# Two of the 32 exponentials in each attention block, computed on VectorE by a polynomial

## The chip, the cores and the metric

The kernel runs on one core of one Trainium2 chip. The metric is the device time of one execution in microseconds (us), the lower the better. Three runs of the kernel before took 1523.89, 1523.95 and 1524.58 us; the median is 1523.95 us. A separate execution was recorded by the hardware profiler; all instruction times below are from that one.

## The reference, cut to what matters

Two attention layers over 2048 tokens with 32 heads of 18 dimensions; their outputs are put side by side.

```python
# A: 32 query heads, one shared key head and one shared value head, no mask
q = (x @ wq) -> [32, 2048, 18];  k = x @ wk;  v = x @ wv            # k, v: [2048, 18]
p = softmax(q @ k.T * 18 ** -0.5);  a = (p @ v, heads joined) @ wo

# B: 32 full heads, four segments of 512 tokens, causal inside a segment
logits = qs @ ks.T * 18 ** -0.5 + mask;  p = softmax(logits)
o = g * (phi(qs) @ M) / (phi(qs) @ z) + (1 - g) * (p @ vs)           # M, z: from earlier segments
b = (o, heads joined) @ wo
out = concatenate([a, b], axis=-1)                                   # float32
```

The change concerns the exponential of A's softmax: 32 heads x 2048 queries x 2048 keys.

## The kernel before, in words

**Stages.** The first 330 us compute projections (queries, keys, values of A and B), bounds that are subtracted inside the exponentials, and B's memory; they write their results to DRAM. The rest, which the change is in, is the attention stage, then a short output stage.

**Blocks and pairs.** An A block is four heads (`hg`) of one chunk of 512 queries (`c`); there are 4 x 8 = 32 of them. Inside a block the loop runs over 16 tiles of 128 keys (`kt`) and, for each, over two *pairs* of heads (`pr`), so a block has 32 pairs. For one pair, `scores` (L715) issues two TensorE matmuls that run side by side on two halves of the rows (L726) and fill one PSUM tile `E` of 128 keys x 2 heads x 512 queries; then one ScalarE instruction (L727) takes the exponential of all 128 x 1024 values into an SBUF tile `P`. `products` (L747) multiplies `P` by the values: for one key tile and one half of the queries (`hf`) it issues four matmuls, one for each head, side by side in four column groups (L761). They add up in one PSUM tile `O`. The sums of the exponentials come out as an extra column of the values. A B block is the same with 3 key tiles, six pairs, narrower ones, and a GpSimd `affine_select` (L741) that cuts off the future.

**PSUM.** There are three `E` tiles (`psE`, L558), handed out in turn: pair i can be filled only when pair i-3 has been read. `O` and `F` have one tile each (`psO`, L559).

**Turns.** TensorE, ScalarE and VectorE execute in the order in which the program issues their work (L843); the order of DMAs on the SyncE queue (SP) and of GpSimd's work is left to the framework. The loop at L854 runs *turns*. A turn issues the scores (and exponentials) of three pairs, one step of the output projection (`run_fill(1)`: four matmuls, L648, into `F`), and the products that belong to the pairs of two turns before. An A block has ten turns of three pairs and one turn, the last, of two; a B block has two turns. There are 352 + 64 = 416 turns. After every fifth step of the projection VectorE copies `F` to SBUF (`osb`, L672), and TensorE needs that copy done before the next step. When a block's products are complete, VectorE copies `O` out (`oe`, L770), and TensorE needs that copy done before the next block's first products.

**Steps that follow a finished chunk.** When all heads of a chunk (A) or a segment (B) are through, `finish` (L801) puts a chain into the list `later`: read the sums back from DRAM (`sums`), take reciprocals on VectorE (`inverses`, L609), load the unnormalized heads and the broadcast reciprocals (`load_heads`, L615), multiply on VectorE (`weigh`, L628). When five such head groups are weighed, the chunk's output projection joins the list `fill`: 60 steps. `due` (L793) executes at most one entry of `later` in a turn. Eight projections are made; the steps that are left when the turns are over are executed after them (L876), and the last chunk's (L889, L895) after that.

## Time and profile before

| | |
|---|---|
| three runs, us | 1523.89, 1523.95, 1524.58 |
| the profiled execution, us | 1525.33 |
| its span on the core, us | 1523.6 |
| TensorE (PE) matmul busy | 1474.2 us, 97% of the span |
| ScalarE (ACT) busy | 1234.7 us, 81% |
| VectorE (DVE) busy | 316.6 us, 21% |
| GpSimd (POOL) busy | 119.3 us, 8% |
| granted TensorE clock | 0.992 over the whole span, 1.00 from 345 to 1480 us |
| window 400 to 1400 us: ACT busy | 98% (980.5 of 1000 us) |
| window 400 to 1400 us: DVE busy | 11% (114.0 of 1000 us) |

How to read it: a row of the group view names the line, the engine, the operation, the tiles written and read, and how often it ran; then the busy time of the group in us (overlaps counted once), the mean duration of one in ns, and the idle time of the engine ahead of the group with what ended it. ScalarE's instructions overlap a little, so their mean duration is longer than their spacing. "PEld" is the load of a matmul's weights, the first thing that a matmul does, so a wait of TensorE shows there. A float32 matmul stands as two instructions in the trace; the score matmuls as one. TensorE's busy share counts overlapped matmuls from start to modelled end and is no measure of its spare time. The timeline view gives start, duration, engine, line and, in brackets, the idle time before a row.

### The profile page before, as it was taken

The page shows a single profiled execution, that of the slowest core. Times are in us where ns is not written, and L with a number is a line of the kernel's source. Part 1 is how long each engine was busy: PE and PEld are TensorE (multiplying, and loading weights), DVE is VectorE, ACT ScalarE, POOL GpSimd, SP SyncE. Part 2 cuts the span into 40 slices and gives each one's busy share as a digit, 9 for nine tenths or more (in the row PEclk, how much of TensorE's full clock was granted, in tenths as well). Part 3 has the DMA queues.
Part 4 walks back from the last instruction along what each step waited for, and adds up shares of the span by engine and source line. Part 5 has one row for each costly group of instructions (what it writes and reads, how often), then busy time and mean ns, then how long its engine had stood idle before and what let it go on. Part 6 is the DMA issues. An engine that isn't in the chain of part 4 may idle for free.

```text
span 1523.6 us, 40356 instructions
## 1 busy us (share of the span) xinstructions
PE 1474.2 (97%) x17540; PEld 840.1 (55%) x17540; DVE 316.6 (21%) x607; ACT 1234.7 (81%) x1456; POOL 119.3 (8%) x221
## 2 busy tenths in 40 slices
PE   8989999999999999999999999999999999999998
PEld 5668878754444555545555454555554444444454
DVE  6564673530011001211000001112012100100011
ACT  3333334259999999999999999999999999999950
POOL 0030000002121111001001010111100000000000
PEclk9989999999999999999999999999999999999999
DMA  6775643456464243432332213342322111010011
GB/s 196 232 234 175 188 153 128 139 169 185 128 187 134 59 135 108 152 101 71 95 101 69 89 51 103 105 144 73 102 90 77 53 41 47 27 52 16 32 64 60
DMA packets 87983, 166.29 MB, mean 109 GB/s; under 512 B 12480, under 2 KB 21242, under 8 KB 87626
## 3 DMA queue, kind: packets, MB, share of 16 engines
q1 hardware_dynamic: 81510, 157.82, 33.4%
q10 hardware_dynamic: 6291, 5.85, 1.2%
q8 instruction: 138, 2.26, 0.6%
q14 instruction: 44, 0.35, 0.1%
HBM read 96.15 MB, written 67.49 MB: 107 GB/s over the span
## 4 chain that ended last, share of the span: by engine, by line
PE 64%; ACT 7%; DMA 3%; issue 3%; SPq 1%; DVE 0%; ACTq 0%; DVEq 0%
PE O L761 28%; PE E L726 21%; PE F L648 12%; ACT P L727 5%; PE E L734 3%; ACT P L737 2%; DMA stB<-qB 1%; PE E L648 1%; DMA woA<-a_wo 1%; DMA stB<-shB 0%; SPq L577 0%; DMA stA<-qA 0%; DVE osb L672 0%; DMA oB<-oe 0%; DMA stB<-ones_d 0%
## 5 line engine op out<-in xcount | busy, mean ns | idle before, releaser
L727 ACT ACTIVATE P<-E 128x1024 f32<-128x1024 f32 x1024 | 958.7, 1040 | 16.5 <-PE E L726 4.7
L761 PE MATMUL O<-P,VA 128*32 128x256 f32 x8192 | 509.3, 380 | 0.1
L726 PE MATMUL E<-stA,kstA 56*128 56x512 f32 x1920 | 367.7, 457 | 9.9 <-ACT P L727 7.4
L761 PEld LDWEIGHTS O<-P,VA 128*32 128x32 f32 x8192 | 261.4, 110 | 148.0 <-issue 10.1
L726 PEld LDWEIGHTS E<-stA,kstA 56*128 56x128 f32 x1920 | 154.4, 184 | 244.5 <-ACT P L727 239.1
L737 ACT ACTIVATE P<-E 128x768 f32<-128x768 f32 (+1 forms) x192 | 155.2, 898 | 8.4 <-PE E L734 7.2
L672 DVE COPY osb<-F 128x192 f32<-128x192 f32 x84 | 30.0, 358 | 594.9 <-PE F L648 594.9
L741 POOL TENSOR_SCALAR_AFFINE_SELECT P<-P 128x256 f32<-128x256 f32 (+1 forms) x192 | 94.6, 493 | 666.6 <-ACT P L737 663.4
L770 DVE COPY oe<-O 128x512 f32<-128x512 f32 x64 | 44.3, 692 | 405.5 <-PE O L761 348.8
L648 PE MATMUL F<-woB,o 126*32 126x192 f32 (+1 forms) x1920 | 127.0, 338 | 0.0
L648 PE MATMUL F<-woA,o 126*32 126x192 f32 (+2 forms) x1480 | 88.7, 337 | 6.1 <-DVE osb L672 6.1
L101 ACT CAST qp<-pj 126x512 fp32r<-126x512 f32 (+1 forms) x56 | 32.6, 584 | 64.7 <-DVE kmB L351 48.4
L761 PE MATMUL O<-P,vseg 128*32 128x256 f32 (+2 forms) x1536 | 81.5, 344 | 0.3 <-POOL P L741 0.2
L199 PE MATMUL pj<-xh,wBh 128*126 128x512 f32 x180 | 74.6, 419 | 3.4 <-DVE xh L171 3.4
L199 PE MATMUL pj<-xh,wBl 128*126 128x512 f32 x180 | 73.2, 406 | 0.0
L734 PE MATMUL E<-stB 56*128 56x256 f32 (+3 forms) x512 | 66.8, 354 | 5.6 <-ACT P L737 3.9
L648 PEld LDWEIGHTS F<-woB,o 126*32 126x32 f32 (+1 forms) x1920 | 38.5, 108 | 58.6 <-issue 53.8
L734 PEld LDWEIGHTS E<-stB 56*128 56x128 f32 x512 | 40.5, 184 | 40.7 <-ACT P L737 16.4
L761 PEld LDWEIGHTS O<-P,vseg 128*32 128x32 f32 x1536 | 48.2, 109 | 25.5 <-issue 2.7
L199 PE MATMUL pj<-xl,wBh 128*126 128x512 f32 x144 | 60.3, 419 | 0.0
L648 PEld LDWEIGHTS F<-woA,o 126*32 126x32 f32 (+1 forms) x1480 | 34.6, 108 | 43.6 <-issue 26.6
L102 DVE TENSOR_TENSOR qp<-pj,qp 126x512 fp32r<-126x512 f32 (+1 forms) x56 | 38.2, 686 | 55.7 <-ACT qp L101 55.5
(124 smaller groups left out, 998.7 us busy)
## 6 DMA issues: line engine op xcount, KB each, us to landing
stB<-kB SPq DMA_DIRECT2D x96, 144.0 KB
stB<-qB SPq DMA_DIRECT2D x32, 288.0 KB
stA<-qA SPq DMA_DIRECT2D x30, 288.0 KB
oA<-oe SPq DMA_DIRECT2D x32, 256.0 KB
oB<-oe SPq DMA_DIRECT2D x32, 256.0 KB
qA<-qp SPq DMA_DIRECT2D x16, 504.0 KB
kB<-qp SPq DMA_DIRECT2D x16, 504.0 KB
qB<-qp SPq DMA_DIRECT2D x16, 504.0 KB
```

Source lines behind the costliest of these rows:

```text
L101: nc.scalar.copy(qp[:R, 0, :n], src)
L102: nc.vector.tensor_tensor(qp[:R, 1, :n], src, qp[:R, 0, :n].bitcast(F32), op=ALU.subtract)
L199: nc.tensor.matmul(dst, w[:, c0 : c0 + M], x, start=i == 0, stop=i == len(ops) - 1)
L648: nc.tensor.matmul(dst[32 * j : 32 * j + 32], parts[ab, c][: RT[t], t, r0 : r0 + 32], wo[ab][: RT[t], t, c0 : c0 + n], start=start, stop=stop,
L672: nc.vector.tensor_copy(osb[:, cs], pf[:, :192])
L726: nc.tensor.matmul(e[:, j], kstA[rows, 128 * kt : 128 * kt + 128], st[rows, h, :], start=True, stop=True)
L727: nc.scalar.activation(p, e, AF.Exp, scale=SCALE)
L734: nc.tensor.matmul(e[:, j, c0 : c0 + 512 - 128 * k], st[rows, 4 + h, ks], st[rows, h, 128 * k :], start=True, stop=True)
L737: nc.scalar.activation(p[:, :, :n], e[:, :, :n], AF.Exp, scale=SCALE)
L741: nc.gpsimd.affine_select(diag, diag, pattern=[[0, 2], [0, m], [1, 128]], base=0, channel_multiplier=-1, compare_op=ALU.is_ge, fill=0.0)
L761: nc.tensor.matmul(o[32 * j : 32 * j + 32, q0 : q0 + n], v, ps_[j // 2][:, j % 2, p0 : p0 + n], start=kt == hf == 0, stop=kt == last and h ...
L770: nc.vector.tensor_copy(osb, o)
```

## The change

In each A block the pairs (key tile 1, pair 0) and (key tile 8, pair 1), numbers 2 and 17 of the block's 32 counted from 0, are taken from ScalarE. VectorE computes their exponential: one instruction reads `E`, scales by log2(e) and limits from below (this frees `E`), and eight more, on SBUF, round to an integer n, form the fraction, evaluate a polynomial of degree five, and multiply by 2^n, which is made from integer bits. The eight stand in a list `slow`, and the loop issues two in a turn, fewer when `due` executed something costly in that turn. The products of these pairs are put at positions 9 and 15 of the block's key order for that pair of heads (`LATE`); in pair 0 the products of key tiles 2 to 9 and in pair 1 those of key tiles 9 to 15 move one position ahead to fill the gap.

Beside this: the tiles of `load_heads` have three buffers instead of four and `vseg` one instead of two (its load is issued when the segment before has its last products); `due` executes up to two entries in a turn, one of them costly at most, and in turns of B too; heads are loaded one by one while fewer than three are held; the B blocks of segments 2 and 3 stand at other places among the A blocks (`after`).

```diff
@@ -42,6 +42,15 @@
 BKEYS = [[(0, 0)], [(1, 0)], [(2, 0), (3, 256)]]
 BHALF = [[(0, 0, 0, 256), (0, 256, 256, 256)], [(1, 0, 128, 192), (1, 192, 320, 192)], [(2, 0, 256, 256), (3, 256, 384, 128)]]
+
+
+LOG2 = SCALE * 1.4426950408889634
+ROUND = 1.5 * 2.0 ** 23
+POLY = [753.2113037109375, 522.0861206054688, 180.93731689453125, 41.808597564697266, 7.287727355957031]
+C5_BITS = 984482944.0
+
+BY_DVE = ((1, 0), (8, 1))
+LATE = (9, 15)
 QALL = [(slice(0, 36, 2), 0), (slice(1, 36, 2), 1), (slice(36, 54), 0)]
 CA = 618
@@ -614,9 +623,9 @@
     def load_heads(ab, c, t):
         o_d, r_d = (oA, rA) if ab == "A" else (oB, rB)
-        tiles = [pa.tile([128, C], F32, name=n, bufs=4) for n in ("oc", "rb")]
+        tiles = [pa.tile([128, C], F32, name=n, bufs=3) for n in ("oc", "rb")]
         if ab == "B" and c > 0:
-            tiles += [pa.tile([128, C], F32, name=n, bufs=4) for n in ("nb", "rb2")]
+            tiles += [pa.tile([128, C], F32, name=n, bufs=3) for n in ("nb", "rb2")]
         lo, n, R = H0[t], HT[t], RT[t]
         nc.sync.dma_start(tiles[0][:R], o_d[c][lo : lo + n, 1:VW, :])
         nc.sync.dma_start(tiles[1][:R], r_d[c][lo : lo + n, None, :].to_broadcast([n, DH, C]))
@@ -694,7 +703,7 @@
     blocksA = [("A", c, hg) for c in range(NCH) for hg in range(8)]
     blocksB = [[("B", s, 2 * h8), ("B", s, 2 * h8 + 1)] for s in range(NSEG) for h8 in range(4)]
-    after = [0, 0, 1, 1, 2, 3, 4, 5, 8, 10, 12, 14, 16, 17, 18, 19]
+    after = [0, 0, 1, 1, 2, 3, 4, 5, 8, 9, 10, 12, 16, 17, 18, 20]
     blocks = []
     for n, b in enumerate(blocksA):
         blocks.append(b)
@@ -707,10 +716,26 @@
     stacks, vseg, state = {}, {}, {}
     def load_vseg(s):
-        v = pa.tile([128, 4, H * VW + 13], F32, name="vseg", bufs=2)
+        v = pa.tile([128, 4, H * VW + 13], F32, name="vseg", bufs=1)
         nc.sync.dma_start(v[:, :, : H * VW], vB[s].rearrange("(i p) c -> p i c", p=128))
         nc.gpsimd.memset(v[:, :, H * VW :], 0.0)
         vseg[s] = v
+
+    slow = []
+
+    def exponentials(p, e):
+
+        n = pp.tile([128, 2, 512], F32, name="n", bufs=1)
+        q = pp.tile([128, 2, 512], F32, name="q", bufs=1)
+        v = nc.vector
+        v.tensor_scalar(p, e, LOG2, -116.0, op0=ALU.mult, op1=ALU.max)
+        slow.append((p, lambda: v.tensor_scalar(n, p, ROUND, ROUND, op0=ALU.add, op1=ALU.subtract)))
+        slow.append((p, lambda: v.tensor_tensor(p, p, n, op=ALU.subtract)))
+        slow.append((p, lambda: v.scalar_tensor_tensor(q, p, POLY[4], p, op0=ALU.add, op1=ALU.mult)))
+        for a in POLY[3:0:-1]:
+            slow.append((p, lambda a=a: v.scalar_tensor_tensor(q, q, a, p, op0=ALU.add, op1=ALU.mult)))
+        slow.append((p, lambda: v.tensor_scalar(n.bitcast(I32), n, 2.0 ** 23, C5_BITS, op0=ALU.mult, op1=ALU.add)))
+        slow.append((p, lambda: v.scalar_tensor_tensor(p, q, POLY[0], n, op0=ALU.add, op1=ALU.mult)))
     def scores(it, pr):
@@ -718,13 +743,17 @@
         st = stacks[ab, c, hg // 2]
         h = 2 * (hg % 2) + pr
         e = psE.tile([128, 2, 512], F32, name="E")
-        p = pp.tile([128, 2, 512], F32, name="P", bufs=PBUFS)
-        state.setdefault(it, []).append(p)
+        dve = ab == "A" and (kt, pr) in BY_DVE
+        p = pp.tile([128, 2, 512], F32, name="PD" if dve else "P", bufs=2 if dve else PBUFS)
+        state[it, pr] = p
         if ab == "A":
             for j, r0 in enumerate(HALF):
                 rows = slice(r0, r0 + KR)
                 nc.tensor.matmul(e[:, j], kstA[rows, 128 * kt : 128 * kt + 128], st[rows, h, :], start=True, stop=True)
-            nc.scalar.activation(p, e, AF.Exp, scale=SCALE)
+            if dve:
+                exponentials(p, e)
+            else:
+                nc.scalar.activation(p, e, AF.Exp, scale=SCALE)
             return
         n = 512 - 128 * kt if kt < 2 else 384
         for k, c0 in BKEYS[kt]:
@@ -744,16 +773,19 @@
     acc = {}
-    def products(it, hf):
-
-        ab, c, hg, kt = it
-        if kt == hf == 0:
+    def products(b, m, hf):
+
+
+        ab, c, hg = b
+        if m == hf == 0:
             acc[0] = psO.tile([128, C], F32, name="O")
         o = acc[0]
-        ps_ = state.pop(it) if hf else state[it]
-        last = NKT - 1 if ab == "A" else 2
-        k, p0, q0, n = (kt, 256 * hf, 256 * hf, 256) if ab == "A" else BHALF[kt][hf]
+        last = (NKT - 1 if ab == "A" else 2) == m
         for j in range(4):
+            kt = turn_of[j // 2][m] if ab == "A" else m
+            p = state[b + (kt,), j // 2]
+            assert all(x[0] is not p for x in slow)
+            k, p0, q0, n = (kt, 256 * hf, 256 * hf, 256) if ab == "A" else BHALF[kt][hf]
             if ab == "A":
                 v = VA[:, VW * kt : VW * kt + 32]
             else:
@@ -761,11 +793,11 @@
             nc.tensor.matmul(
                 o[32 * j : 32 * j + 32, q0 : q0 + n],
                 v,
-                ps_[j // 2][:, j % 2, p0 : p0 + n],
-                start=kt == hf == 0,
-                stop=kt == last and hf == 1,
+                p[:, j % 2, p0 : p0 + n],
+                start=m == hf == 0,
+                stop=last and hf == 1,
             )
-        if kt == last and hf:
+        if last and hf:
             osb = pa.tile([128, C], F32, name="oe", bufs=2)
             nc.vector.tensor_copy(osb, o)
             od = oA if ab == "A" else oB
@@ -773,6 +805,15 @@
             return hg
         return None
+
+    turn_of = []
+    for pr in range(2):
+        ks = [kt for kt in range(NKT) if (kt, pr) not in BY_DVE]
+        for (kt, p_), pos in zip(BY_DVE, LATE):
+            if p_ == pr:
+                ks.insert(pos, kt)
+        turn_of.append(ks)
+
     keys = {ab: list(dict.fromkeys((ab, c, hg // 2) for a_, c, hg in blocks if a_ == ab)) for ab in "AB"}
     def prefetch(ab, upto):
@@ -784,19 +825,22 @@
     prefetch("B", 1)
     load_vseg(0)
     FILL = 60
-    later, weighed, loaded = [], {}, [0]
-
-    def at(k, ready, step):
-        later.append((k, ready, step))
+    later, weighed, loaded, summing = [], {}, [0], set()
+
+    def at(k, cost, ready, step):
+        later.append((k, cost, ready, step))
         later.sort(key=lambda e: e[0])
-    def due(k, n=1):
-
+    def due(k, most=2):
+
+        cost = 0
         for e in [e for e in later if e[0] <= k]:
-            if n and e[1]():
+            if most and not (cost and e[1]) and e[2]():
                 later.remove(e)
-                e[2](k)
-                n -= 1
+                e[3](k)
+                cost += e[1]
+                most -= 1
+        return cost
     def finish(k, ab, c, hg):
@@ -805,22 +849,29 @@
         box = {}
         weighed.setdefault((ab, c), 0)
         last = (ab, c) == blocks[-1][:2]
-        d1, d2, step = (2, 3, 1) if last else (2, 5, 1) if ab == "A" or c == 0 else (2, 7, 2)
+        mem = ab == "B" and c > 0
+        d1, d2 = (2, 3) if last else (2, 5)
         def begin(k):
-            loaded[0] += len(ts)
+            summing.add(hg)
             box[0] = sums(ab, c, lo, hi)
-            at(k + d1, lambda: True, inv)
+            at(k + d1, 0, lambda: True, inv)
         def inv(k):
             inverses(ab, c, lo, hi, box[0])
+            summing.remove(hg)
             for t in ts:
-                box[t, t] = load_heads(ab, c, t)
-                at(
-                    k + d2 + step * (t - ts[0]),
-                    lambda: (ab, c) in parts or len(parts) - filled[0] // FILL < 2,
-                    lambda k, t=t: heads(k, t),
-                )
+                at(k, 0, lambda: loaded[0] < 3, lambda k, t=t: load(k, t))
+
+        def load(k, t):
+            loaded[0] += 1
+            box[t, t] = load_heads(ab, c, t)
+            at(
+                k + d2,
+                3 if mem else 1,
+                lambda: (ab, c) in parts or len(parts) - filled[0] // FILL < 2,
+                lambda k, t=t: heads(k, t),
+            )
         def heads(k, t):
             if (ab, c) not in parts:
@@ -829,9 +880,9 @@
             loaded[0] -= 1
             weighed[ab, c] += 1
             if weighed[ab, c] == 5 and not last:
-                at(k + 1, lambda: True, lambda k: fill.append(out_proj(ab, c)))
-
-        at(k + (0 if last else 1), lambda: loaded[0] + len(ts) <= 4, begin)
+                at(k + 1, 0, lambda: True, lambda k: fill.append(out_proj(ab, c)))
+
+        at(k + (0 if last else 1), 0, lambda: hg not in summing and loaded[0] < 3, begin)
     def split(n, cut):
@@ -856,12 +907,16 @@
                 scores(its[n], pr)
             run_fill(1)
             for n, hf in prods[k - 2] if k > 1 else []:
-                it = its[n]
-                hg = products(it, hf)
+                ab, c = its[n][:2]
+                hg = products(its[n][:3], its[n][3], hf)
                 if hg in (6, 7):
-                    finish(k, it[0], it[1], hg)
-            if k > 1 and its[prods[k - 2][-1][0]][0] == "A":
-                due(k)
+                    finish(k, ab, c, hg)
+                if hg == 7 and ab == "B" and c + 1 < NSEG:
+                    load_vseg(c + 1)
+            cost = due(k)
+            for _ in range(2 - min(cost, 2)):
+                if slow:
+                    slow.pop(0)[1]()
             for n, pr in turns[k] if k < len(turns) else []:
                 it = its[n]
                 ab = it[0]
@@ -869,8 +924,6 @@
                     prefetch(ab, keys[ab].index((ab, it[1], it[2] // 2)) + 2)
                     if it in (("A", 0, 0, 4), ("A", 0, 2, 4)):
                         load_wo(*(("A", a_wo) if it[2] == 0 else ("B", b_wo)))
-                    if ab == "B" and it[2] == 4 and it[3] == 0 and it[1] + 1 < NSEG:
-                        load_vseg(it[1] + 1)
         ab, c = blocks[-1][:2]
         while fill:
```

## The prediction

> **What bounds the kernel now.** I read the page first (busy time by engine, groups), then the windows view and the timelines of TensorE, ScalarE and VectorE inside one A block, then the waits. In the groups ScalarE looks like the bound:
>
> ```profile
> PE 1474.2 (97%) x17540; PEld 840.1 (55%) x17540; DVE 316.6 (21%) x607; ACT 1234.7 (81%) x1456; POOL 119.3 (8%) x221
> L727 ACT ACTIVATE P<-E 128x1024 f32<-128x1024 f32 x1024 | 958.7, 1040 | 16.5 <-PE E L726 4.7
> ```
>
> Between 400 and 1400 us it is busy 98% of the time, and the waits view has TensorE's weight loads waiting for it:
>
> ```profile
> PEld E L726 <- ACT P L727: 259.9, 637, 1.4
> ```
>
> The timelines correct this picture. The first row below is ScalarE at 395 us, where turns have no projection step yet, the second at 1300 us, where each has one:
>
> ```profile
> 395.13 11.15 ACT L727 ACTIVATE P<-E 128x1024 f32<-128x1024 f32 x12
> ...
> 1299.52 13.34 ACT L727 ACTIVATE P<-E 128x1024 f32<-128x1024 f32 x14
> ```
>
> One instruction lasts 1.04 us and overlaps the next, so the spacing is (11.15 - 1.04)/11 = 0.92 us in the first and (13.34 - 1.03)/13 = 0.947 us in the second. At 1300 us ScalarE is thus not at its own pace, though it looks fully busy: its overlap hides the waits. TensorE waits too:
>
> ```profile
> 1303.71 0.30 PEld L726 LDWEIGHTS E<-stA,kstA 56*128 56x128 f32 x4 [0.41 <-ACT P L727]
> 1304.44 0.19 PEld L726 LDWEIGHTS E<-stA,kstA 56*128 56x128 f32 x2 [0.44 <-ACT P L727]
> ...
> 1306.63 0.30 PEld L726 LDWEIGHTS E<-stA,kstA 56*128 56x128 f32 x4 [0.41 <-ACT P L727]
> 1307.21 0.19 PEld L726 LDWEIGHTS E<-stA,kstA 56*128 56x128 f32 x2 [0.29 <-ACT P L727]
> ...
> 1309.41 0.30 PEld L726 LDWEIGHTS E<-stA,kstA 56*128 56x128 f32 x4 [0.41 <-ACT P L727]
> ```
>
> Turns start at 1303.71, 1306.63, 1309.41: they last 2.92 and 2.78 us in turn. The third score (1304.44) waits, then come projection and products, and the next turn's first score starts 2.19 us later. Only then does ScalarE get new work. This is a **loop** through three E tiles: third score to next turn's first score 2.19, its matmul 0.50, two ScalarE spacings 1.82, the third exponential 1.03, and the E tile of the third score after next is free. That makes 5.54; the two turns last 5.70, so 0.16 is left for two handovers. The loop, not either engine, sets 2.85 us a turn. Without a projection step it is 0.35 us shorter a turn, and ScalarE's own pace rules: 3 x 0.92 = 2.75 us.
>
> TensorE alone: a block's last turn, of two pairs, takes 1.98 us (1312.32 to 1314.31 in the timeline) and waits for nothing. A third pair adds a score (0.22) and two waves of products (0.43): 2.63 us. The upper bound is the 2.78 us turn. I take 2.63, as a turn that waits for nothing is the nearer row.
>
> **The change, part by part.**
>
> *64 exponentials leave ScalarE* (2 x 32 blocks). Their spacing is 64 x 0.947 = 61 us, but little of it lies on the end. Pairs 2 and 17 are each the third pair of their turn (turns 0 and 5 of a block). In such a turn ScalarE has two pairs and then waits for the next turn's first score, which TensorE can't issue sooner than 2.19 us after the third. What goes is the loop through that one turn: the next turn can follow at TensorE's 2.63. The loop then closes over the following two turns again, 5.70 together. Between two freed turns the 5.70s fit wholly into an even number of turns, and leave one of 2.63 instead of 2.85 in an odd number: at most 0.22 us. Walking all pairs of a block through with these durations gives 30.42 us before (the trace has 1375.27 to 1405.73, 30.46) and turns of 2.80, 2.62, 3.06, 2.74, 2.94, 2.74, 2.62, 3.06, 2.74, 2.94, 1.98 after: a gain of 0.15. In blocks without projection steps two turns around a freed one take 2.19 - 0.35 + 0.50 + 1.82 + 1.03 + 0.16 = 5.35 instead of 5.48: 0.12, twice a block. With 28 and 4 blocks: 28 x 0.15 + 4 x 0.24 = **-5.2 us**. Bounds: 28 x 0 at 2.78 for TensorE alone, and the 61 us of the first rival.
>
> *VectorE's nine instructions a pair.* None of 1024 elements stands in the trace. The read of E: a PSUM copy takes 692 ns for 512 (L770) and 358 for 192 (L672), 1.04 ns an element, so 1.23 us. The eight on SBUF depend on one another, as here:
>
> ```profile
> 618.81 0.74 DVE L639 SCALAR_TENSOR_TENSOR oc<-oc,omg,rb 126x512 f32<-126x512 f32 x1
> 619.47 0.69 DVE L641 TENSOR_TENSOR nb<-nb,rb 126x512 f32<-126x512 f32 x1
> 620.19 0.69 DVE L642 TENSOR_TENSOR o<-oc,nb 126x512 f32<-126x512 f32 x1
> ```
>
> 0.72 us from one to the next that needs it, with 512 more elements 1.25. Six have two tensor inputs: 7.5. The two with one input lie between 0.77 (the 512-element cast on SBUF takes 507 ns, L171, against 692 from PSUM: half the price an element) and 1.25. A pair costs 10.3 to 11.3 us, a block up to 22.6 of its 30.3, beside other engines' work. On the path is only the release of E: 0.6 us after the third score the read can start, at 1.9 us E is free, TensorE wants it at 2.63: 0.7 us to spare. Between the two reads lie five turns, 14.0 us; 11.3 + `oe` 0.69 + one `osb` 0.36 = 12.4 fit. So **0**, with the second rival as the upper end.
>
> *Products.* The same number. One key tile ahead, they need at the latest the turn before's third exponential; that turn's E tile is what this turn's third score has just waited for. The late ones come over 6 turns after their read. 0.
>
> *Waits ahead of VectorE's queue.* 16 reciprocals and 40 weighings wait for DMAs, and a read of E may now stand behind one. Between 480 and 1470 us VectorE waited 27.7 us for DMAs (18.4, 6.3 and 3.0 in the waits view), counted from when it had nothing else to do. Bounds 0 and 27.7; I take **+0.6**, since weighings come five turns (14 us) after their load and only those that meet one of two turns in eleven matter.
>
> *Loads.* The one `vseg` is reloaded (1216 KB) after a segment's last products; the next segment is at least one A block, 29 us, away; at the 59 to 187 GB/s that the page's slices show moved there it takes 7 to 21 us. SP has the next stacks behind it, fetched a stack ahead. Three head buffers instead of four, loads that enter SP one by one: the weighings keep five turns. 0; if a load is late, it joins the wait above.
>
> *The projection starts earlier.* I followed the two lists (`later`, `fill`) turn by turn. Before, 63 turns run with an empty `fill`, and 65 steps are left at the end; the trace agrees (first step in the 63rd turn's place at 497 us; the chain's end shows pieces of five steps, 13 of them). After, `due` takes two entries and works in B's turns, so segment 0's projection begins at turn 55; turn 115 is empty; 56 turns in all and 58 steps left. In the tail,
>
> ```profile
> 1495.67 1.88 PE F L648 x40
> 1497.57 0.37 DVE osb L672
> 1497.94 0.04 issue
> 1497.99 1.83 PE F L648 x40
> ```
>
> five steps take 2.32 us: seven fewer are -3.2. Seven turns become 2.85 instead of 2.75: +0.7. Together **-2.5**.
>
> Sum: -5.2 + 0.6 - 2.5 = -7.1 us: span 1523.6 to 1516.5, and with the 1.7 us around it the profiled execution's 1525.3 to 1518.2. That execution lies 1.4 us above the median, from which I get 1523.95 - 7.1 = **1517**.
>
> **Rivals.**
> 1. *ScalarE is the bound after all.* For: 98% busy. [...] Against: the spacing of 0.947 where 0.92 is possible. Its price is 61 us and TensorE alone would just allow it (10 x 2.63 + 1.98 = 28.3 a block): 1461 us. Chance 0.06. [...]
> 2. *VectorE's queue is late with the reads of E* (slower). Place: turn 5, whose read stands behind turn 0's eight instructions. It decides when one takes over (14.0 + 0.7 - 1.23 - 1.05)/8 = 1.55 us, or when waits for DMAs use the same spare time. At 1.6 us the read is 0.4 late in each block: 32 x 0.4 = 13 us: 1530. For: no row has such instructions back to back for long; a freed turn also wants VectorE faster. Against: 1.25 from rows. Chance 0.22.
> 3. *The loop gives nothing* (TensorE alone needs 2.78) and only the tail gains: -2.5 + 0.6: 1522. Chance 0.17.
> 4. *GpSimd's selects (L741) come late.* 14 A blocks follow B's, and VectorE starts its eight while the last select is due. If each waits for one of them, 14 x 1.25 = 17 us: 1534. Against: TensorE waited 0.2 us for selects, and the products follow over 2 us later. Chance 0.03. [...]
>
> **The numbers.** My forecast holds 0.52, from 1511 to 1520.5. A measurement tells 0.2%, 3 us, from no change. Faster by more: forecast and rival 1, 0.58. Within: rival 3, 0.17. Slower: rivals 2 and 4, 0.25. The range, 1509 to 1530, leaves out rivals 1 and 4 and nearly half of rival 2.
>
> **What would show it.** ScalarE 60 us less busy, its idle time up by nearly as much, behind TensorE; turns after a freed one short (2.6) and the next long (3.06); VectorE 70 to 80% busy inside A blocks with instructions of 1.2 us; the read of E ended before TensorE wants the tile; first projection step near 475 us; twelve pieces in the tail. Wrong: turns all near 2.6, or TensorE waiting for VectorE at L726 or L648.

## The result, and the profile after

The changed kernel takes **1529.41 us** (median of 6 runs, 1527.08 to 1532.81) against 1523.92 us (6 runs, 1522.54 to 1525.46) in the same sitting: ratio 1.0037, 95% interval 1.0024 to 1.0051. It is slower by 5.5 us, where 7 us faster were forecast. The profiled execution took 1527.08 us (span 1525.4), the fastest of the six: 1.8 us more span than before.

From the page after (busy time by engine, then groups: line, engine, tiles, count | busy us, mean ns | idle us before, releaser):

```profile
PE 1461.6 (96%) x17540; PEld 840.6 (55%) x17540; DVE 935.8 (61%) x1183; ACT 1180.2 (77%) x1392; POOL 120.6 (8%) x221
...
L756 ACT ACTIVATE P<-E 128x1024 f32<-128x1024 f32 x960 | 904.8, 1035 | 75.6 <-PE E L752 69.2
...
L731 DVE TENSOR_SCALAR PD<-E 128x1024 f32<-128x1024 f32 x64 | 78.1, 1220 | 110.9 <-PE E L752 103.6
L733 DVE TENSOR_TENSOR PD<-PD,n 128x1024 f32<-128x1024 f32 x64 | 78.4, 1225 | 2.1
```

ScalarE is 54.5 us less busy, and its idle time ahead of these exponentials rose by about as much, from 16.5 to 75.6 us; of that, 4.7 and now 69.2 us were spent waiting for the scores (L726, now L752). VectorE's read of E and its instructions with two inputs cost what was forecast, 1.22 us.

**Where nothing disturbs, the change gains.** TensorE's weight loads in one late A block; turns start at the rows with the tile E and x4 or x6:

```profile
1381.46 0.30 PEld L752 LDWEIGHTS E<-stA,kstA 56*128 56x128 f32 x4 [0.41 <-ACT P L756]
...
1384.20 0.53 PEld L752 LDWEIGHTS E<-stA,kstA 56*128 56x128 f32 x6 [0.41 <-ACT P L756]
...
1386.86 0.30 PEld L752 LDWEIGHTS E<-stA,kstA 56*128 56x128 f32 x4 [0.41 <-ACT P L756]
1387.65 0.19 PEld L752 LDWEIGHTS E<-stA,kstA 56*128 56x128 f32 x2 [0.50 <-ACT P L756]
...
1389.84 0.30 PEld L752 LDWEIGHTS E<-stA,kstA 56*128 56x128 f32 x4 [0.41 <-ACT P L756]
```

The eleven turns last 2.74 2.66 2.98 2.76 2.88 2.83 2.65 2.99 2.75 2.89 1.98 us. The turn after a freed pair (1384.20, six loads in one row: the third score waits for nothing) is 2.66, the next 2.98, as the walk forecast. What it did not forecast: this block lasts 30.11 instead of 30.46 us. The second and third turn together, the fourth and fifth, the seventh and eighth, the ninth and tenth (2.66 + 2.98, 2.76 + 2.88, 2.65 + 2.99, 2.75 + 2.89) take 5.64 us each, where the same turns took 5.69 to 5.71 before. But for the first, the blocks after the first chunk gain 0.2 to 0.5 us each.

**The loss lies in chunk 0.** Against before, six blocks are longer, all of them before 700 us: (B,0,2) +4.0 (this block began 4.2 us earlier than before, so this evens out); (A,0,2) +5.2; (A,0,3) +2.6; (A,0,6) +1.7; (A,0,7) +6.1; (A,1,0) +0.7. Between 380 and 1470 us, twelve turns last over 3.4 us, 18.5 us more than 2.8 us each; before, none does. Two of them (434.08 and 478.38, 6.0 us of the 18.5) wait for the copy of `O`, of which more under x1; eight (6.7 us) come up again under x18. The longest, 7.87 us, starts at 631.74. First VectorE, then TensorE's weight loads:

```profile
630.34 0.75 DVE L648 SCALAR_TENSOR_TENSOR oc<-oc,omg,rb 126x512 f32<-126x512 f32 x1 [1.87 <-DMA rb<-rB]
632.93 0.69 DVE L650 TENSOR_TENSOR nb<-nb,rb 126x512 f32<-126x512 f32 x1 [1.83 <-DMA rb<-rdB]
633.65 0.69 DVE L651 TENSOR_TENSOR o<-oc,nb 126x512 f32<-126x512 f32 x1
634.26 1.22 DVE L731 TENSOR_SCALAR PD<-E 128x1024 f32<-128x1024 f32 x1
```

```profile
631.74 0.30 PEld L752 LDWEIGHTS E<-stA,kstA 56*128 56x128 f32 x4 [0.41 <-ACT P L756]
635.53 0.28 PEld L752 LDWEIGHTS E<-stA,kstA 56*128 56x128 f32 x2 [3.49 <-DVE PD L731]
```

A weighing (L648 to L651) waits for its two broadcast loads, 1.87 and 1.83 us; the read of E (L731), ready for 4 us, stands behind it in VectorE's queue; and TensorE's third score needs that E tile: 3.49 us without work. That is the sign of failure that the prediction had named. Why the loads are late stands in SP's queue of the same execution:

```profile
625.41 0.34 SPq L130 DMA_DIRECT2D stB<-qB  x1
627.02 0.77 SPq L630 DMA_DIRECT2D oc<-oB  x1
628.82 0.74 SPq L631 DMA_DIRECT2D rb<-rB  x1
630.26 0.34 SPq L633 DMA_DIRECT2D nb<-numB  x1
631.01 0.77 SPq L634 DMA_DIRECT2D rb<-rdB  x1
```

One head's four loads enter one by one, the first two with over 1 us of standstill ahead of each. What ends the standstills stands in SP's own waits view for 615 to 640 us (us in total, times, longest):

```profile
SPq L630 <- DMA rb<-rdB: 2.3, 2, 1.2
SPq L631 <- DMA oc<-oB: 1.0, 1, 1.0
SPq L633 <- DMA rb<-rB: 0.7, 1, 0.7
```

They end when earlier transfers land, not when a buffer comes free. By the landings in this trace, each of the four loads went out within 0.1 us of the landing of the transfer eight places ahead of it: `rb<-rB` at 628.82 when the `oc<-oB` of 619.25 us had landed (628.81), 9.6 us after that was issued; the other three when the `rb<-rdB` of 618.46, the `rb<-rB` of 620.03 and the `nb<-numB` of 620.80 had (626.96, 630.25, 630.99). The weighing that needs them reaches VectorE's head at 628.47 us, before `rb<-rB` has even entered the queue.

After the stall TensorE loses time once more, in the clock. The windows view of the same execution (start:end, length, busy time of PE, PEld, DVE, ACT, POOL, then the granted clock):

```profile
433.50:436.90 3.40, 2.08 (x22) 0.82 (x14) 0.97 (x2) 3.40 (x5) 0.14 (x1) 0.99 0.71 240
437.00:440.00 3.00, 2.76 (x26) 1.02 (x26) 2.54 (x3) 1.28 (x2) 0.00 (x0) 0.50 0.21 56
...
632.00:636.00 4.00, 0.94 (x6) 0.33 (x4) 3.04 (x5) 1.94 (x2) 0.00 (x0) 0.85 0.56 190
636.00:640.00 4.00, 4.00 (x36) 1.85 (x36) 1.81 (x3) 1.02 (x1) 0.00 (x0) 0.50 0.55 179
640.00:645.00 5.00, 5.00 (x64) 2.61 (x66) 4.90 (x6) 4.16 (x5) 0.00 (x0) 0.83 0.57 191
645.00:650.00 5.00, 4.93 (x71) 2.35 (x64) 3.72 (x6) 4.97 (x6) 0.00 (x0) 1.00 0.18 63
```

After the stall the clock is 0.50 for four microseconds and 0.83 for the next five, with TensorE busy all the time: 4 x 0.50 + 5 x 0.17 = 2.9 us of work lost on top of the stall. The turns show it as time: from the third score to the next turn's first 4.08 us pass (635.53 to 639.61) instead of 2.19, and the turn after lasts 3.54 us instead of some 2.65. The clock is at half at 437 us too, in the first of the two turns that wait for `O`: there after 3.4 us in which TensorE was busy for 2.08, with no standstill over 1.5 us. After 635.53 us some 6 us of work pass until it is back at 1.00 (0.50 from 640 to 641 us, 0.67 from 641 to 642, 1.00 from 642 to 643).

### The profile page after: what moved, and what is told of

Same layout as the page of the kernel before. It is cut to its first block, busy times and chain, and to the rows that moved or that the text cites. A ratio compares the mean times of both kernels' runs of the same rounds, so it can differ in the third digit from the quotient of the medians.

```text
span 1525.4 us, 40379 instructions
## 1 busy us (share of the span) xinstructions
PE 1461.6 (96%) x17540; PEld 840.6 (55%) x17540; DVE 935.8 (61%) x1183; ACT 1180.2 (77%) x1392; POOL 120.6 (8%) x221
## 4 chain that ended last, share of the span: by engine, by line
PE 56%; ACT 12%; DMA 5%; issue 3%; DVE 1%; SPq 0%; ACTq 0%; DVEq 0%
PE O L793 25%; PE E L752 17%; PE F L657 11%; ACT P L756 10%; PE E L763 3%; ACT P L766 2%; DMA stB<-qB 1%; DMA rb<-rdB 1%; PE E L657 1%; DMA oA<-oe 1%; DMA woA<-a_wo 1%; DMA rB<-sm 0%; DMA stA<-qA 0%; DMA oB<-oe 0%; DVE PD L731 0%
## 5 line engine op out<-in xcount | busy, mean ns | idle before, releaser
L756 ACT ACTIVATE P<-E 128x1024 f32<-128x1024 f32 x960 | 904.8, 1035 | 75.6 <-PE E L752 69.2
L752 PE MATMUL E<-stA,kstA 56*128 56x512 f32 x1920 | 355.7, 452 | 20.3 <-ACT P L756 12.4
L752 PEld LDWEIGHTS E<-stA,kstA 56*128 56x128 f32 x1920 | 156.0, 185 | 234.2 <-ACT P L756 214.7
L736 DVE SCALAR_TENSOR_TENSOR q<-q,PD 128x1024 f32<-128x1024 f32 x192 | 234.8, 1223 | 6.0
L731 DVE TENSOR_SCALAR PD<-E 128x1024 f32<-128x1024 f32 x64 | 78.1, 1220 | 110.9 <-PE E L752 103.6
L733 DVE TENSOR_TENSOR PD<-PD,n 128x1024 f32<-128x1024 f32 x64 | 78.4, 1225 | 2.1
L738 DVE SCALAR_TENSOR_TENSOR PD<-q,n 128x1024 f32<-128x1024 f32 x64 | 78.4, 1224 | 2.0
L734 DVE SCALAR_TENSOR_TENSOR q<-PD 128x1024 f32<-128x1024 f32 x64 | 77.9, 1218 | 0.9
L657 PEld LDWEIGHTS F<-woB,o 126*32 126x32 f32 (+1 forms) x1920 | 37.8, 108 | 63.2 <-issue 58.9
```

Source lines behind the costliest of these rows:

```text
L657: nc.tensor.matmul(dst[32 * j : 32 * j + 32], parts[ab, c][: RT[t], t, r0 : r0 + 32], wo[ab][: RT[t], t, c0 : c0 + n], start=start, stop=stop,
L731: v.tensor_scalar(p, e, LOG2, -116.0, op0=ALU.mult, op1=ALU.max)
L733: slow.append((p, lambda: v.tensor_tensor(p, p, n, op=ALU.subtract)))
L734: slow.append((p, lambda: v.scalar_tensor_tensor(q, p, POLY[4], p, op0=ALU.add, op1=ALU.mult)))
L736: slow.append((p, lambda a=a: v.scalar_tensor_tensor(q, q, a, p, op0=ALU.add, op1=ALU.mult)))
L738: slow.append((p, lambda: v.scalar_tensor_tensor(p, q, POLY[0], n, op0=ALU.add, op1=ALU.mult)))
```

## The experiments

All edits are to the changed kernel. "Schedule" below means all of the change but the two pairs and the order of their products.

### The schedule without the pairs (x1), and the pairs without VectorE (x2)

x1:

```diff
-BY_DVE = ((1, 0), (8, 1))
-LATE = (9, 15)
+BY_DVE = ()
+LATE = ()
```

> All of the change but the two pairs: every exponential stays on ScalarE and the products keep their order. Theory Q (the loss is made where a read of E stands in VectorE's queue behind a reciprocal or a weighing that waits for a DMA): no read of E, nothing to hold up, so only the projection's earlier start is left, -2.5 us: 1521.5 us, between 1519 and 1524. Rival S (the loss comes from the other edits: three head buffers, one vseg, the moved B blocks, the busier list of due steps): the loss of some 18 us stays and the gain of the pairs is gone: over 1530 us.

Measured 1537.09 us (1532.57 to 1537.97), ratio 1.0083 (1.0067 to 1.0098). **My first theory fell**: without one read of E the schedule alone loses 13 us. Blocks (A,0,3) and (A,0,7) are 9.5 and 5.2 us longer, the others as before. The 10.96 us turn in (A,0,3), TensorE, VectorE and the SP queue in turn:

```profile
477.69 0.53 PE L657 MATMUL F<-woB,o 126*32 126x192 f32 x8
484.29 2.79 PE L793 MATMUL O<-P,VA 128*32 128x256 f32 x24 [6.06 <-DVE oe L802]
```

```profile
471.74 1.74 DVE L646 SCALAR_TENSOR_TENSOR o<-oc,omg,rb 126x512 f32<-126x512 f32 x2
483.54 0.69 DVE L802 COPY oe<-O 128x512 f32<-128x512 f32 x1 [10.06 <-DMA oA<-oe]
```

```profile
466.44 5.46 SPq L140 DMA_DIRECT2D stB<-shB  x4
473.57 2.50 SPq L586 DMA_DIRECT2D stB<-kB  x3
...
478.91 0.25 SPq L587 DMA_DIRECT2D stB<-ones_d  x1
479.26 0.35 SPq L804 DMA_DIRECT2D oA<-oe  x1
```

The products need `O` copied out; that copy needs its buffer stored; and the store (L804, 479.26) entered SP's queue only behind a whole stack of B, issued from 464.79 to 479.16 us. In the changed kernel the loads of the same stack waited for head loads to land: between 466 and 480 us 1.8 us for `rb<-rB` and 1.4 for `oc<-oB` at L140, 1.2 for `rb<-rB` at L586. The two turns there at 434.08 and 478.38 us are of this kind: the copy waits 2.4 and 3.9 us for its buffer's store, and the products 1.5 and 2.3 us for the copy. In (A,0,7) of x1 it is an `osb` copy (639.13) behind weighings that wait 1.52 us for `rb<-rB` and 1.62 for `rb<-rdB`; TensorE waits 3.2 us.

x2 leaves out the exponentials of pairs 2 and 17; their products read a tile of ones:

```diff
+    fixed = pp.tile([128, 2, 512], F32, name="fixed", bufs=1)
+    nc.gpsimd.memset(fixed, 1.0)
...
-        p = pp.tile([128, 2, 512], F32, name="PD" if dve else "P", bufs=2 if dve else PBUFS)
+        p = fixed if dve else pp.tile([128, 2, 512], F32, name="P", bufs=PBUFS)
...
-            if dve:
-                exponentials(p, e)
-            else:
+            if not dve:
```

> Leaves out the exponentials of pairs 2 and 17 of every A block altogether: nobody reads their E tile, and their products read one tile of ones. It measures what the removal of 64 exponentials from ScalarE is worth at most. Loop theory (three E tiles, third score to third score; an undisturbed block gained 0.3 to 0.45 us in the changed kernel): 32 x 0.4 + 2.5 = 15 us less than before, 1509 us, between 1504 and 1513. Rival A (ScalarE is the bound): 64 x 0.947 = 61 us less, about 1461 us.

Measured 1523.95 us (1520.08 to 1525.75), ratio 1.0005 (0.9996 to 1.0015), 13 us below x1. So the pairs do gain, and ScalarE is not the bound: with the same 64 exponentials gone and nothing in their place, 13 us come back of the 61 that they occupied. The 98% of busy time that I weighed in rival 1 is no sign of a bound here: consecutive exponentials, 1.04 us each, overlap, and they still do at the 0.947 us spacing that has waits in it, so the busy share hides the waits.

### Steps further behind their loads (x3, x5, x7, x8)

`d1` is the number of turns from the load of the sums to the reciprocals, `d2` from the load of heads to the weighing. x3:

```diff
-        d1, d2 = (2, 3) if last else (2, 5)
+        d1, d2 = (2, 3) if last else (5, 8)
```

> The changed kernel with the reciprocals five turns after the read of the sums instead of two, and the weighings eight turns after their load instead of five, so that the DMAs have landed before VectorE comes to the instruction. Theory Q: the 18 us that six blocks lost come back, the projection starts eight turns later (+3): 1514 us, between 1510 and 1518, with no turn over 4 us in the first two chunks. Rivals S and W (VectorE's eight instructions themselves make it late): 1529 us or 3 more.

Measured **1511.81 us** (1510.33 to 1512.38), ratio 0.9925 (0.9911 to 0.9938): faster than both kernels. No instruction of VectorE waits for `sm` or `rb` any more. TensorE's waits for the read of E between 400 and 1470 us, after:

```profile
PEld E L752 <- DVE PD L731: 5.2, 3, 3.5
```

and with the later steps:

```profile
PEld E L752 <- DVE PD L731: 0.2, 1, 0.2
```

x5 is x3 with `BY_DVE = ()`, `LATE = ()`: what do the later steps give by themselves?

> The later steps (five and eight turns) with every exponential on ScalarE. Revised theory H (the loss is made by the chain of head steps: a load enters SP's queue in the turn of the weighing that frees its buffer, a weighing enters VectorE's queue before its DMA has landed, and all that stands behind them on SP and VectorE, the copies of O and F as well as reads of E, comes late): without early steps nothing is lost, and with 64 turns without a projection step against 63 before nothing is gained: 1523.5 us, between 1521 and 1526. What the pairs are worth is then its distance from the kernel with later steps and pairs, 11 to 12 us. Rival S (three buffers, one vseg or the moved B blocks cost by themselves): 1530 us or more.

Measured 1525.33 us (1522.88 to 1525.93), ratio 1.0004 (0.9994 to 1.0013). With later steps the schedule costs nothing, so the one `vseg`, the moved B blocks and the three buffers are not by themselves what loses time in x1. The pairs, on a schedule that doesn't hurt, are worth 1525.3 - 1511.8 = **13.5 us** (12.0 by the ratios, as the two ran in different sittings).

x7 is x1 with `(5, 5)`, only the reciprocals later; x8 is x1 with `(2, 8)`, only the weighings later.

> The kernel with the schedule edits alone, with the reciprocals five turns after the read of the sums instead of two; the weighings stay five turns after their load. If the reciprocals' waits (9.9 and 7.2 us) make the loss: 1523 to 1525 us. Theory H, by which the long turns at 476 and 635 us stand behind loads and weighings: most of the loss stays, 1531 to 1537 us.

> The kernel with the schedule edits alone, with the weighings eight turns after their load instead of five; the reciprocals stay two turns after the sums. Theory H: 1522 to 1526 us. If the reciprocals make the loss: 1533 to 1537 us.

Measured 1523.66 us (1520.48 to 1526.63), ratio 1.0000 (0.9988 to 1.0011), and 1528.61 us (1523.96 to 1529.64), ratio 1.0030 (1.0018 to 1.0043). Either delay alone cures much of the schedule's loss, measured against x6 of the same sitting (below, 1537.69, as x1): all 14.0 us of it, and 9.1. The theory that only the weighings matter fell. The two cures overlap (their sum is more than there is to cure); that later reciprocals also load the heads later, and so spread the steps over more turns, is a guess.

### Which part of the schedule (x4, x6, x15, x16)

x4 keeps the pairs to chunks 1 to 3 (`dve = ab == "A" and c > 0 and (kt, pr) in BY_DVE`, and the old key order in chunk 0).

> The changed kernel with the two pairs on VectorE in chunks 1 to 3 only; the eight blocks of chunk 0, where the long turns stood, are as before. Theory Q: 24 blocks gain 0.37, the earlier projection 2.5, block 0 of chunk 1 may lose 0.7: 1513 us, between 1510 and 1517. Rival W: the loss goes with the number of pairs, three quarters of +5.5: 1528 us. Rival S: 1529 us or more.

Measured 1525.38 us (1522.16 to 1527.91), ratio 1.0021 (1.0012 to 1.0030). Without a read of E in chunk 0, (A,0,3) and (A,0,7) still lose 8.7 and 4.2 us: the reads are not the cause of the loss, they are one of the things that stand behind it.

x6 is x1 with four buffers in `load_heads` and `loaded[0] < 4`:

> The kernel with the schedule edits alone (two and five turns, no pairs), with four head buffers and up to four heads held, instead of three. If three buffers make the loss (the fourth head's load blocks SP until a weighing is done): the 14 us go, 1522 us. If the distance of five turns from load to weighing makes it, the loads only come sooner and together: 1530 to 1537 us. Theory H has both in it and expects part: 1527 to 1533 us.

Measured 1537.69 us (1535.45 to 1538.49), ratio 1.0084 (1.0066 to 1.0101), as x1: the fourth buffer is not missed, which fits the waits of SP's queue for transfers rather than for buffers.

x15 is x1 with one entry of the list a turn, in A's turns only, as before:

```diff
-            cost = due(k)
+            cost = due(k, 1) if k > 1 and its[prods[k - 2][-1][0]][0] == "A" else 0
```

> The schedule edits alone (no pairs, two and five turns), with one entry of the list a turn and only in turns that end in products of A, as in the kernel before. If the busier list (two entries, also in B's turns) makes the 14 us: 1523 us, between 1520 and 1527. If not: 1531 to 1538 us.

x16 is x1 with the second head group held until a weighing of the first is done (`(hg == 6 or weighed[ab, c] >= 1) and ...` in the condition of `begin`):

> The schedule edits alone, with the sums of a chunk's second group (its last four heads) read only when one head group of the first is weighed, as in the kernel before, where four held buffers kept them back. If the two groups' chains, running into each other on SP, make the 14 us: 1523 us, between 1520 and 1527. If not: 1531 to 1538 us.

Measured 1526.22 us (1521.00 to 1528.67), ratio 1.0015 (1.0005 to 1.0024), and 1530.66 us (1527.28 to 1530.78), ratio 1.0038 (1.0024 to 1.0052). The busier list is the larger part: by the ratios, one entry a turn takes back 10 us of x1's 13, the later second group 7.

### The pairs on the old schedule (x12, x17)

Would the pairs have gained had nothing else been changed? x12 has them with before's `finish`, `due`, `after` and four head buffers; the SBUF for this comes from `PBUFS = 7` instead of 9. The loop always issues two of the eight instructions.

> The two pairs on VectorE and the moved products, with the kernel before's list of steps, its order of blocks and its four head buffers; one vseg as in the change, and seven P tiles instead of nine to make room. If the loss lies in the new steps and not in the pairs: before less the pairs' 13 us, 1511 us, up to 1514 where a read of E meets an old step that waits. If reads of E behind any waiting step make the loss: 1520 to 1530 us. If seven P tiles hold ScalarE up, its idle time behind products shows it.

Measured 1616.99 us (1614.49 to 1619.27), ratio 1.0616 (1.0599 to 1.0634). This tells nothing of the schedule: the waits view shows ScalarE out of tiles, which before never happened (with B's exponentials the waits are 125.6 us).

```profile
ACT P L756 <- PE O L793: 80.7, 132, 3.2
```

x17 has eight `P` tiles instead (three buffers for `nb` and `rb2` pay for it).

> The pairs with the kernel before's list of steps and order of blocks, with eight P tiles (seven held ScalarE up for 123 us behind products) and three buffers for two of B's four head tiles. If eight are enough: 1511 to 1514 us, which would lay the whole loss on the new steps. If ScalarE still waits behind products by tens of us, the run says nothing on the steps but that the pairs need their P tiles.

Measured 1544.97 us (1542.57 to 1545.69), ratio 1.0137 (1.0120 to 1.0154). Those waits shrank to 13.5 us, but 13 turns last over 3.4 us (17.1 us more than 2.8 each). In most of them a read of E or a copy of `F` comes late on VectorE: the old steps, too, put reciprocals and weighings ahead of them. Before, VectorE could wait there for up to 10.3 us at a time at hardly any cost to TensorE. But the blocks of chunks 1 and 3 without long turns also lack the gain: they are 0.2 us shorter to 0.4 longer than before, where x3's are 0.2 to 0.5 shorter. So x17 shows that the old steps hurt the pairs, not how much of its 21 us is theirs and how much that of eight tiles.

### One pair (x13, x14)

Both are x3 with one pair: pair 2 alone (x13), pair 17 alone (x14).

> Later steps; only pair 2 of each A block on VectorE. By the prediction's account of the loop (an even number of turns between two freed ones gives nothing) one freed turn in eleven gives as much as two: 1512 us. If each freed turn gives its own share: half of 13.5 us, 1518.5 us.

> Later steps; only pair 17 of each A block on VectorE. By the prediction's walk through a block this one alone gives nothing in blocks with projection steps: 1524 to 1525 us. If each freed turn gives its own share: 1518.5 us.

Measured 1520.56 us (1517.35 to 1524.29), ratio 0.9981 (0.9969 to 0.9993), and 1521.72 us (1519.74 to 1523.07), ratio 0.9985 (0.9975 to 0.9995). In chunks 1 to 3 a block gains 0.15 us on average with pair 2 and 0.06 with pair 17, but 0.37 with both. My account by even and odd turns fell: the gain of two freed pairs is more than the sum of theirs one by one.

### E tiles in turn (x18, x19), and no VectorE work at x3's times (x9, x20)

In the changed kernel seven turns of chunk 0 and one of the first block of chunk 1 last 3.5 to 3.9 us, with the third score waiting some 1.3 us for an exponential of its own turn. TensorE's weight loads in (A,0,2):

```profile
449.83 0.19 PEld L752 LDWEIGHTS E<-stA,kstA 56*128 56x128 f32 x2 [1.32 <-ACT P L756]
...
453.37 0.19 PEld L752 LDWEIGHTS E<-stA,kstA 56*128 56x128 f32 x2 [1.38 <-ACT P L756]
```

I conclude that the program runs there on two of the three E tiles: the framework, which hands them out, left out the one whose read is late. x18 hands them out strictly in turn (three names, one buffer each):

```diff
-    psE = ctx.enter_context(tc.tile_pool(name="psE", bufs=3, space=PSUM))
+    psE = ctx.enter_context(tc.tile_pool(name="psE", bufs=1, space=PSUM))
+    given = [0]
...
-        e = psE.tile([128, 2, 512], F32, name="E")
+        e = psE.tile([128, 2, 512], F32, name="E" + "abc"[given[0] % 3])
+        given[0] += 1
```

> The changed kernel, with the three E tiles handed out strictly in turn (three names with one buffer each). In the changed kernel the turns from 448.22 to 462.24 us last 3.47, 3.53, 3.48, 3.54 us instead of some 2.74, those at 613.72 and 617.52 us 3.80 and 3.86 instead of 2.85, the one at 651.54 us 3.67 instead of 2.75: in each the third score waits until its own turn's first exponential is done, so it writes that pair's tile, and one of the three tiles lies unused. Together these seven turns cost 3.1 + 1.9 + 0.9 = 5.9 us. Theory K (the tile set aside is a cost of its own): it goes, and 1529.4 becomes about 1523.5. Rival L (it is only another form of the late read): in turn, the third score at 449.83 us would have to wait for the read that ends at 451.21 us, 2.4 us later than in an undisturbed turn against the 3.0 us that the four turns cost, and the one at 615.33 us for a read that ends at 616.27, 2.0 against 1.9; the time stays within 1.5 us of 1529.4: 1528 to 1530. Under both, the long turn at 631.74 us (7.87) stays.

Measured 1529.79 us (1519.72 to 1534.78), ratio 1.0032 (1.0014 to 1.0051): as the changed kernel, rival L. The waits are now on the reads themselves. VectorE, then TensorE's weight loads:

```profile
447.49 0.25 DVE L619 RECIPROCAL sm<-sm 128x16 f32<-128x16 f32 x1 [3.73 <-DMA sm<-oB]
447.66 1.16 DVE L732 TENSOR_SCALAR PD<-Ea 128x1024 f32<-128x1024 f32 x1
...
650.40 0.95 DVE L619 RECIPROCAL sm<-sm 112x128 f32<-112x128 f32 x1 [3.88 <-DMA sm<-oA]
```

```profile
445.83 0.18 PEld L754 LDWEIGHTS Eb<-stA,kstA 56*128 56x128 f32 x2 [0.41 <-ACT P L758]
445.94 0.19 PEld L754 LDWEIGHTS Ec<-stA,kstA 56*128 56x128 f32 x2
448.88 0.29 PEld L754 LDWEIGHTS Ea<-stA,kstA 56*128 56x128 f32 x2 [2.75 <-DVE PD L732]
```

Reciprocals wait 3.7 and 3.9 us for `sm`, the reads start when they are done, and at 448.88 a third score has waited 2.75 us for the read of `Ea` that began at 447.66.

x19 does the same to x17, the pairs on the old schedule:

> The pairs with the schedule of the kernel before (the kernel of x17), with the three E tiles handed out strictly in turn. There eight turns run on two tiles (3.5 us without, 3.86 us with a projection step, instead of 2.75 and 2.85). Theory K: 4 x 0.75 + 4 x 1.0 = 7 us less than its 1545: 1538. Rival L: within 2 us of 1545. Both expect it slower than the kernel before, since the reads of E still stand behind reciprocals and weighings that wait for their transfers.

Measured 1542.30 us (1541.39 to 1544.13), ratio 1.0118 (1.0103 to 1.0133): 2.7 us of x17's 21, nearer to L. The tile left out is mostly another form of the late read.

x9 is x3 with x2's edit, and x20 the same with the tiles in turn: like x2, they leave out the two pairs' exponentials.

> Later steps (five and eight turns); leaves out the exponentials of pairs 2 and 17 as x2_no_read does (their products read a tile of ones). If VectorE's nine instructions a pair cost nothing once nothing holds them up: the same as with them, 1512 us, between 1510 and 1514. If they cost something everywhere: under 1508 us. If ScalarE were the bound: 1525 - 61 = 1464 us.

> The kernel of x9 (steps five and eight turns after their loads; the exponentials of pairs 2 and 17 left out, their products read a tile of ones), with the E tiles handed out strictly in turn. In x9 a tile that nobody reads was given out again at once, so its order of tiles was another than in x3. If VectorE's nine instructions a pair are hidden and the order of tiles made x9 slow, it takes what x3 took: 1511 to 1513. If they are hidden and x9's excess came from transfers in the first blocks, as x9: 1515 to 1517. If VectorE's work costs something in x3, less than x3's 1511.8 by over 1.5 us: below 1510.

Measured 1515.82 us (1514.85 to 1517.20), ratio 0.9954 (0.9938 to 0.9971), and 1517.33 us (1515.56 to 1517.80), ratio 0.9952 (0.9939 to 0.9965). Without VectorE's work it is not faster than x3 but slower, by some 4 us, nearly all of it in (B,0,2) and (A,0,2), each some 2 us longer than in x3; from chunk 1 on the blocks last as long as x3's within 0.1 us. So VectorE's nine instructions cost nothing when its queue doesn't wait. Why the first blocks are better with them is open.

## Why the prediction was wrong, point by point

- **What bounds the kernel: right.** The loop through three E tiles sets the turn, not ScalarE (x2: 13 us back of 61).
- **64 exponentials leave ScalarE, -5.2: right in kind, too small.** By x5 and x3 the pairs are worth 12 to 13.5 us, some 0.4 a block where 0.15 was walked (there, two spacings of 0.92 are 1.84 and not 1.82, which moves little). The short and long turns came as walked (2.66 and 2.98, forecast 2.62 and 3.06). The rule that an even number of turns between freed ones gives nothing failed: with both pairs freed, the turns between them, taken two by two, got 0.06 us shorter as well, and one pair alone gives 0.15 or 0.06 a block (x13, x14). What shortens them is not known.
- **VectorE's instructions, 0: right.** 1.22 us for the read and for each with two inputs, 0.69 for the two with one; some 10.1 us a pair, forecast 10.3 to 11.3. The forecast's lower price for one input, 0.77, came from a mean of 507 ns at L171 that a few long casts pull up; the median there is 421.
- **Products, 0: right.** In the products TensorE waited once, for 0.2 us, for VectorE's work on the pairs. **Selects (rival 4): rightly put aside.** TensorE waited 0.8 us for selects (0.9 before), and no select ran at the same time as one of VectorE's eight instructions on SBUF, so whether these would hold one up was not tested: that a select waits for one of them, 1.25 us each, was my assumption, and no run shows it. In the changed kernel three selects ran beside a weighing for over 0.3 us, and each time the one that began later took longer than others of its size. One of the three, VectorE, then GpSimd:

```profile
985.03 1.28 DVE L643 TENSOR_TENSOR o<-oc,rb 126x512 f32<-126x512 f32 x2
```

```profile
985.92 0.68 POOL L770 TENSOR_SCALAR_AFFINE_SELECT P<-P 128x256 f32<-128x256 f32 x1 [0.86 <-ACT P L766]
986.83 0.42 POOL L770 TENSOR_SCALAR_AFFINE_SELECT P<-P 128x256 f32<-128x256 f32 x1 [0.24 <-ACT P L766]
```

  The select that began 0.39 us before the weighing's end took 0.68 us, the next of its size 0.42; a reciprocal ran beside it as well, for 0.24 us. In the other two the select came first and kept its 0.42 (980.60) and 0.64 us (474.48, the wider form), and the weighing took longer: 0.86 us at 980.71 where the median of its line is 0.68, and 1.07 at 474.59 where it is 0.75. How much either loses in general three cases don't show.
- **Waits ahead of VectorE's queue, +0.6: this step failed.** I granted that VectorE's 27.7 us of waits could matter, then took "weighings come five turns (14 us) after their load" for enough, and counted only the reads of E. The turns are counted from where the program issues the load; in SP's queue the load stands behind stacks and earlier head loads, and the issues there waited for earlier transfers to land, up to 1.2 us each between 615 and 640 us. In the long turn the weighing was ready before its load had entered the queue. Reciprocals, two turns behind their load, I did not look at; they made VectorE wait up to 3.9 us.
- **Loads, 0, "if a load is late, it joins the wait above": failed with it.** Two entries a turn, B's turns and loads one by one bunch the chain; x1 puts this at +13 us with no pair at all, through `oe` and `osb` copies and SP's stores. Three buffers for four is indeed 0 (x6).
- **The projection earlier, -2.5: the part that shows is right.** The tail has seven steps fewer (56 projection matmuls in the trace), and from the start of the last turn to the end 55.6 us pass instead of 58.9. The first step stands at 480 us (forecast 475, before 498). What the seven further turns with a step cost was not measured.

In sum, the gain was there and larger than forecast: with steps that come late enough it is 1511.8 us, beyond the forecast. What I took for +0.6 and, in the loads, for 0 was together 1529.4 - 1511.8 = 17.6 us (17.1 by the ratios). Of the rivals, the second came nearest, by its second condition ("waits for DMAs use the same spare time") and not by its price per block: not 0.4 us in 32 blocks but 0.7 to 5.1 us in each of a dozen turns, all but one in chunk 0. That its 1530 lies next to the measured 1529.4 is luck.

**Open** is the exact split of the 13 us among the busier list, the loads one by one and the stores on SP (x7, x8, x15 and x16 overlap), and the 0.06 us.

## What to carry to other kernels

Before work that TensorE waits for is put on an engine with slack, list every instruction of that engine that waits for a DMA: its wait, harmless so far, becomes the wait of all that the program issued behind it (here 3.49 us of TensorE's, behind a weighing's waits of 1.87 and 1.83). Count the distance between load and use from the load's entry into its queue, not from where the program issues it, and look at what the queue's own issues wait for; three more turns made 11 us less out of 5.5 us more here. And test an engine that looks full by leaving work out: a busy share made of overlapping instructions hides waits (98% busy here, and 13 us back of the 61 that were left out).

## What the runs showed of the hardware that I had not expected

A stall of 3.49 us was followed by nearly as much again lost in the clock, 2.9 us: 0.50 for four microseconds, 0.83 for five; and a standstill of under 1.5 us, after two shorter ones, was followed by half clock as well. The runs of a kernel with such stalls also differed much. The twelve of x18 go from 1519.72 us at a mean granted clock of 0.993 to 1534.78 at 0.984, in nearly that order, while the five of x3, in whose trace the clock is not lowered between 400 and 1470 us, lie within 2.1 us at 0.992 to 0.994. The last dozen us of x18's time are thus not one number. That a stall lowers the clock in one run and not in another would explain it; with one trace a kernel, this is not shown.
